# Eight experts and a two-layer product: weight conversion inside the second layer, and one block of rows completed by a one-hot product

## The chip, the cores and the metric

The kernel runs on one core of a Trainium2 chip. The metric is the device time of one execution in microseconds (us), given as the median of several runs. Beside the runs there is one execution recorded by the hardware profiler; all rows shown below come from that one.

## The reference, cut to what matters

Three parts follow one another. Attention keeps the 32 largest scores of each row (4 batches, 8 heads, 576 positions, head size 64) and gives a matrix `x` of 2304 rows by 512. Then each row with a positive skip score goes through the one of eight experts that its gate picks, and the last part is a product with two large matrices:

```python
for e in range(E):                       # E = 8, w1[e]: 512 x 1024, w2[e]: 1024 x 512
    mask = e_idx == e
    h = np.maximum(xc[mask] @ w1[e], 0.0)
    y[mask] = gate_w[mask, None] * (h @ w2[e])
out[do_compute] = xc + y
...
h = x @ w_in                             # 512 x 2048, float64
g = h * (1.0 / (1.0 + np.exp(-1.702 * h)))
return (g @ w_out).astype(np.float32)    # 2048 x 512, float64
```

`w_in` and `w_out` arrive as 64-bit floats. The kernel has to turn each of their elements into a pair of 32-bit floats, a high part and the rest.

## The kernel before, in words

Within a phase, each engine works through its instructions in the order in which the program writes them; nothing reorders them. A wait of one instruction therefore holds everything behind it on the same engine. Loads are issued by SP's queue, also in program order, and a load waits until the buffer that it fills is free.

**Attention** (lines 127 to 762) ends by writing the rows of `x` to two copies in device memory: XD, which the experts gather from, and X2D, which they scatter their results into and which the last part reads. It also sorts the experts by size and makes for each a list of row numbers, IXS. The four largest experts have up to 192 rows ("long", in two tiles of 128 and 64 rows), the other four up to 128 ("short"). They are taken in turn, long and short alternating: experts 0, 2, 4 and 6 in order of the work are long, 1, 3, 5 and 7 are short.

**An expert** (loop of line 990) goes so. `layer1` (line 922) multiplies the 1024 columns of w1, in eight steps f of 128, with the turned rows xgT. After each step ScalarE (ACT) makes the high part of hb, VectorE (DVE) the low part (line 930), and `step(f)` is called. There are four PSUM buffers `ph` for the eight steps. `step` (line 997) first splits one eighth of w2 into a high part (ACT) and a low part w2l (line 968: POOL in some steps, DVE in the others). In step 0 it has POOL gather the rows of the next expert (line 118). In steps 0 and 4 it scatters finished rows of the expert before (line 958). And it does the conversion of w_in: `split_f64` (line 859) is a generator in three parts. The first part loads a slice of 512 KB, named raw (line 861). The second is three VectorE instructions that put the bits of a 32-bit float together (lines 865 to 867). The third makes the high part on ACT (line 870) and the low part on POOL (line 871). There are sixteen slices of w_in; long experts convert three, short ones one. In step 0 the first two are loaded, and from step 2 on they are converted. There are two buffers for raw, so the third load waits until the first slice has been converted.

After layer 1 come, in program order: the loads of the next expert's w2 (eight pieces, line 106, each waiting until its buffer has been split), the turn of the next expert's rows (line 914, `turn`), and `layer2` (line 935), which multiplies hb with w2 in three products per step for a 128-row tile and two for the 64-row tile. VectorE then adds gate times result to the row (line 948, or 951 to 953 for the 64-row tile). The load of w1 for expert e+1 is written at the start of expert e (line 991), into one of two buffers.

**The seam** (lines 1021 to 1107): the last rows are scattered, two slices of w_out are loaded and converted, the table for the sigmoid is loaded, 31 products without use keep TensorE going (line 1028), and the experts' memory is given back. Then the first 512 rows of X2D are loaded (line 1046), turned by 16 transposes (line 1100) and split into xh and xl (lines 1103 to 1107).

**The product stage** (line 1109) takes the rows in blocks of 512. In each of 16 steps `up` makes phh (line 1067) and splits the activated result, and `down` (line 1082) multiplies the result of the step before with woh and wol. In the first block step f also converts slice f+2 of w_out.

Of the kernel before, what the change touches and what calls it, by code (L numbers as in the profile page):

```python
# [8 lines left out]
F32 = mybir.dt.float32  # L9
F32R = mybir.dt.float32r  # L10
# [19 lines left out]
def body(ctx: ExitStack, tc: tile.TileContext, q, k, v, w_skip, w_gate, w1, w2, w_in, w_out, out):  # L30
    nc = tc.nc
    V, A, G, T, SY = nc.vector, nc.scalar, nc.gpsimd, nc.tensor, nc.sync
    P = 128
# [57 lines left out]
    def load_w1(e):  # L91
        w1t = ew.tile([P, KC, F], F32, name="w1t")
        if isinstance(e, int):
            SY.dma_start(w1t, w1[e].rearrange("(c p) f -> p c f", p=P))
        else:
            SY.dma_start(w1t, w1[bass.ds(e, 1), :, :].rearrange("o (c p) f -> p (o c) f", p=P))
        return w1t
# [14 lines left out]
    own = cst.tile([P, 1], I32, name="own")  # L112
    V.tensor_copy(own, iop)
    IX0 = cst.tile([P, 2], I32, name="IX0")
    ZD = dram.tile([P, 8], F32, name="ZD")

    def fetch_rows(xg, ix, src=XD):
# [9 lines left out]
    with ExitStack() as ph:  # L127
# [116 lines left out]
        def warm(k):  # L244
            for _ in range(k):
                T.matmul(Y, ones[:, :P], ones, start=True, stop=True)
# [610 lines left out]
            first_rows()  # L857

    def split_f64(pool, src, hi, lo, queue=SY):
        raw = pool.tile([P, DFF // 4, 2], I32, name="raw")  # L860
        queue.dma_start(raw.rearrange("p n w -> p (n w)"), src.bitcast(I32))
        yield
        t = pool.tile([P, DFF // 4], I32, name="t")
        u = pool.tile([P, DFF // 4], I32, name="u")
        V.tensor_scalar(t, raw[:, :, 1], 3, 0x3FFFFFF8, op0=ALU.logical_shift_left, op1=ALU.bitwise_and)
        V.scalar_tensor_tensor(u, raw[:, :, 1], -0x40000000, t, op0=ALU.bitwise_and, op1=ALU.bitwise_or)
        V.scalar_tensor_tensor(t, raw[:, :, 0], 29, u, op0=ALU.logical_shift_right, op1=ALU.bitwise_or)
        yield
        wf = t.bitcast(F32)
        A.activation(hi, wf, AF.Copy)  # L870
        G.tensor_tensor(lo, wf, hi.bitcast(F32), op=ALU.subtract)
        yield
# [13 lines left out]
    with ExitStack() as ph:  # L886
# [21 lines left out]
        def turn(tiles, xgs):  # L908
            xgT = mp.tile([P, KC, NS], F32, name="xgT")
            o = 0  # L910
            for (_, rows), xg in zip(tiles, xgs):
                pt = pT.tile([P, KC, P], F32, name="pt")
                for c in range(KC):
                    T.transpose(pt[:, c, :rows], xg[:rows, c * P : (c + 1) * P], ident[:rows, :rows])
                if o:
                    A.activation(xgT[:, :, o : o + rows], pt[:, :, :rows], AF.Copy)
                else:
                    V.tensor_copy(xgT[:, :, :rows], pt[:, :, :rows])
                o += rows
            return xgT  # L920

        def layer1(w1t, xgT, ns, step):
# [9 lines left out]
                step(f)  # L932
            return hb

        def layer2(hb, ws, tiles, xgs):
            for (ix, rows), xg in reversed(list(zip(tiles, xgs))):
                py = pY.tile([P, DM], F32, name="py")
                xo = mp.tile([P, DM], F32, name="xo")
                if rows < P:
                    parts = [(P, 0), (P, 1)]  # L940
                else:
                    parts = [(0, 0), (0, 1), (2 * P, 0)]
                for f in range(FC1):
                    for u, (o, b) in enumerate(parts):
                        T.matmul(py, hb[:, f, o : o + P], ws[b][f], start=(f == 0 and u == 0),  # L945
                                 stop=(f == FC1 - 1 and u == len(parts) - 1))
                if rows == P:
                    V.scalar_tensor_tensor(xo, py, xg[:, DM:], xg[:, :DM], op0=ALU.mult, op1=ALU.add)  # L948
                else:
                    yo = mp.tile([P, DM], F32, name="yo", bufs=1)  # L950
                    A.activation(yo[:rows], py[rows:, :], AF.Copy)
                    V.tensor_tensor(yo[:rows], py[:rows, :], yo[:rows], op=ALU.add)
                    V.scalar_tensor_tensor(xo[:rows], yo[:rows], xg[:rows, DM:], xg[:rows, :DM], op0=ALU.mult, op1=ALU.add)
                late.append((ix, xo[:rows]))
# [18 lines left out]
        for c in range(KC):  # L973
            for u in range(4):
                us = slice(u * DFF // 4, (u + 1) * DFF // 4)
                todo.append(split_f64(wt, w_in[c * P : (c + 1) * P, us], wih[:, c, us], wil[:, c, us],
                                      SY if todo[1:] else A))

        turns = [0, 4, 1, 5, 2, 6, 3, 7]
        slots = []  # L980
# [6 lines left out]
        xgs = x0  # L987
        warm(10)
        nx = turn(slots[0], xgs)
        for e in range(E):  # L990
            w1n = load_w1(who[e + 1]) if e + 1 < E else None
            long = turns[e] < BIGS
            ns = NS if long else P
            convs = [todo.pop(0) for _ in range(1 if e % 2 else 3)]
            ws = ([], [])

            def step(f):
                split_w2(raws, ws, f, long)
                if f == 0:
                    for g in convs[:2]:  # L1000
                        next(g)
                    if e + 1 < E:
                        nxt.append(gather(slots[e + 1]))
                if f in (0, 4) and late:
                    scatter()
                for k, g in enumerate(convs):
                    if f - 2 * k in (2, 3):
                        next(g)
                if f == 4 and len(convs) > 2:
                    next(convs[2])  # L1010

            hs = layer1(w1t, nx, ns, step)
            if e + 1 < E:
                raws = load_w2(who[e + 1])
                nx = turn(slots[e + 1], nxt[-1])
            layer2(hs, ws, slots[e], xgs)
            if e + 1 < E:
                xgs = nxt[-1]
                w1t = w1n

        while late:
            scatter()
        todo = [out_weights(fw, wt) for _ in range(2)]
        for _ in range(3):
            for g in todo:
                next(g)
        A.activation(padf, padf, AF.Sigmoid)
        warm(31)

    ewx.close()  # L1030
    with ExitStack() as ph:
        ph.enter_context(tc.manual_schedule())
        fw = ph.enter_context(tc.tile_pool(name="fw2", bufs=1))
        wt = ph.enter_context(tc.tile_pool(name="wt2", bufs=2))
        fp = ph.enter_context(tc.tile_pool(name="fp", bufs=2))
        pT = ph.enter_context(tc.tile_pool(name="pT", bufs=2, space=PSUM))
        pH = ph.enter_context(tc.tile_pool(name="pH", bufs=2, space=PSUM))
        pO = ph.enter_context(tc.tile_pool(name="pO", bufs=1, space=PSUM))
        todo = [None, None] + [out_weights(fw, wt) for _ in range(2, FC2)]
        blocks = [(t0, min(512, NT - t0)) for t0 in range(0, NT, 512)]  # L1040

        def fetch(b):
            t0, n = blocks[b]
            xr = fp.tile([P, 4, DM], F32, name="xr", bufs=1)
            for t in range(n // P):
                SY.dma_start(xr[:, t, :], X2D[t0 + t * P : t0 + (t + 1) * P, :])  # L1046
            xh = fp.tile([P, KC, 512], F32R, name="xh")
            xl = fp.tile([P, KC, 512], F32R, name="xl")
            return xr, xh, xl

        def flip(b, x, c):
            n = blocks[b][1]
# [38 lines left out]
                    V.tensor_copy(ot, po[t])  # L1091
                SY.dma_start(out[t0 + t * P : t0 + (t + 1) * P, :], ot)

        x = fetch(0)
        for f in range(2, 4):
            next(todo[f])
        pts = [pO.tile([P, DM], F32, name=f"po{c}") for c in range(KC)]
        for t in range(4):
            for c in range(KC):
                T.transpose(pts[c][:, t * P : (t + 1) * P], x[0][:, t, c * P : (c + 1) * P], ident)  # L1100
        for c in range(KC):
            if c == 1:
                V.tensor_copy(x[1][:, c, :], pts[c])
# [1 line left out]
                A.activation(x[1][:, c, :], pts[c], AF.Copy)  # L1105
        for c in range(KC):
            V.tensor_tensor(x[2][:, c, :], pts[c], x[1][:, c, :].bitcast(F32), op=ALU.subtract)
        prev = None
        for b in range(len(blocks)):
            po = [pO.tile([P, DM], F32, name=f"po{t}") for t in range(blocks[b][1] // P)]  # L1110
            for f in range(FC2):
                gs = up(b, x, f)
                if b == 0 and f + 2 < FC2:
                    next(todo[f + 2])
                    next(todo[f + 2])
                    if f + 4 < FC2:
                        next(todo[f + 4])
                if prev:
                    down(*prev)
                    if prev[0] < b:  # L1120
                        flush(prev[0], prev[3])
                prev = (b, f, gs, po)
                if b + 1 < len(blocks):
                    if f == 1:
                        xn = fetch(b + 1)
                    elif f in (6, 8, 10, 12):
                        flip(b + 1, xn, f // 2 - 3)
            if b + 1 < len(blocks):
                x = xn
# [32 lines left out]
```

## Time and profile before

| | us |
|---|---|
| median of 3 runs | 1116.03 (1115.49 to 1120.85) |
| the profiled execution, its own time | 1116.85 |
| its span | 1115.0 |
| TensorE busy (PE) | 1017.0, 91% of the span |
| VectorE busy (DVE) | 706.9, 63% |
| ScalarE busy (ACT) | 622.1, 56% |
| GpSimd busy (POOL) | 449.0, 40% |

The span is what the profiler saw from first to last instruction. The profiler's names are PE for TensorE's products and PEld for its weight loads, DVE, ACT, POOL and SP. An `L` number is a line of the kernel. In an arrow `out<-in` the names are those of the program. A row of a timeline gives start, duration, engine, line, instruction and count; in brackets stand the idle time before it and what ended that. `hb <- ACT` in a wait reads: the instruction that writes hb waited for ACT. "Clk" is the clock granted to TensorE as a share of its full rate. In float32, TensorE's timeline has two records for each product.

### The profile page before, as it was taken

To read this page: it belongs to the slowest core of one execution; us is meant where nothing else is said; L and a number is where in the kernel's file an instruction comes from. 1 tells how busy PE (TensorE), PEld (TensorE's weight loads), DVE (VectorE), ACT (ScalarE), POOL (GpSimd) and SP (SyncE) were. 2 spreads that over 40 slices of the span, in tenths; PEclk is the share of its full clock that TensorE was granted. 3 is DMA by queue.
4 is the path that set the end of the run, shared out by engine and by line. 5 is a ranking of instruction groups with operands and counts; after the bars stand their busy time and mean duration, and the time that the engine had idled before them with its cause. 6 is when DMAs were issued, how large, how long until landed. Compare 5 with 4: busy or idle time off the path is not lost. (4 is left out here: it accounts for less than half of the span.)

```text
span 1115.0 us, 20235 instructions
## 1 busy us (share of the span) xinstructions
PE 1017.0 (91%) x6523; PEld 848.8 (76%) x6523; DVE 706.9 (63%) x3376; ACT 622.1 (56%) x1426; POOL 449.0 (40%) x584
## 2 busy tenths in 40 slices
PE   6899999899999999877879778999999999999998
PEld 3777777787777777765768667688888878888887
DVE  7988889988998899944655666566322223222232
ACT  5999999999999999932233333333222222222232
POOL 4777777767777777713435354222000000000000
PEclk8999999999999999988889889999999999999999
DMA  4211141154111310036677673332100010010010
GB/s 102 48 33 33 32 119 29 36 187 122 37 37 37 83 54 16 2 86 212 225 258 275 231 245 134 136 120 95 59 18 1 19 58 1 1 57 1 0 39 19
DMA packets 98803, 91.86 MB, mean 82 GB/s; under 512 B 71680, under 2 KB 71680, under 8 KB 98688
## 3 DMA queue, kind: packets, MB, share of 16 engines
q1 hardware_dynamic: 96704, 84.17, 24.6%
q0 software_dynamic: 1696, 5.25, 1.4%
q8 instruction: 54, 0.88, 0.3%
q10 hardware_dynamic: 288, 1.05, 0.3%
q14 instruction: 61, 0.50, 0.2%
HBM read 72.38 MB, written 17.05 MB: 80 GB/s over the span
## 5 line engine op out<-in xcount | busy, mean ns | idle before, releaser
L275 DVE MAX8 C<-s 128x8 f32<-128x72 f32 x1152 | 217.9, 221 | 2.2 <-ACT s L268 2.2
L307 POOL TENSOR_TENSOR z<-s,z 128x576 f32<-128x576 f32 x144 | 203.2, 1411 | 4.3 <-ACT z L302 4.0
L1070 DVE TENSOR_TENSOR g<-phh,g 128x512 f32<-128x512 f32 (+1 forms) x80 | 51.1, 638 | 178.8 <-ACT g L1069 178.8
L1069 ACT ACTIVATE g<-phh 128x512 f32<-128x512 f32 (+1 forms) x80 | 44.3, 553 | 168.0 <-PE phh L1067 168.0
L409 PE MATMUL Y<-vn,AT 128*128 128x65 f32 x1024 | 121.4, 272 | 0.0
L409 PEld LDWEIGHTS Y<-vn,AT 128*128 128x128 f32 x1024 | 119.4, 192 | 0.0
L302 ACT ACTIVATE z<-s,T 128x576 f32<-128x576 f32 x144 | 116.4, 808 | 2.8 <-DVE T L291 2.8
L339 ACT ACTIVATE k<-s,BT 128x576 bf16<-128x576 f32 x144 | 115.3, 801 | 0.4
L1082 PE MATMUL po<-woh,gh 128*128 128x512 f32 x288 | 112.7, 391 | 1.9 <-DVE ot L1091 1.7
L353 PE MATMUL pt<-ident,a 128*128 128x128 f32 x576 | 113.1, 283 | 1.2 <-POOL z L307 1.0
L268 ACT ACTIVATE s<-SS 128x576 f32<-128x576 f32 x144 | 96.8, 673 | 30.7 <-PE SS L262 28.6
L1082 PE MATMUL po<-wol,gh 128*128 128x512 f32 x288 | 112.4, 390 | 0.0
L1082 PE MATMUL po<-woh,gl 128*128 128x512 f32 x288 | 112.3, 390 | 0.0
L334 POOL TENSOR_SCALAR a<-s,BT 128x576 f32<-128x576 f32 x144 | 107.3, 745 | 0.5 <-POOL BT L296 0.4
L312 DVE MAX8 z<-z 128x8 f32<-128x576 f32 x144 | 107.0, 743 | 0.0
L354 PE MATMUL pt<-nident,k 128*128 128x128 bf16 x576 | 105.1, 221 | 0.0
L927 PE MATMUL ph<-xgT,w1t 128*128 128x192 f32 (+1 forms) x512 | 76.9, 312 | 17.8 <-DVE hb L930 17.2
L260 PE MATMUL SS<-kT,qT 64*128 64x256 f32 x512 | 73.6, 407 | 19.6 <-ACT s L268 19.6
L353 PEld LDWEIGHTS pt<-ident,a 128*128 128x128 f32 x576 | 83.8, 146 | 9.4 <-POOL z L307 1.2
L342 ACT ACTIVATE AT<-pt 128x512 f32<-128x512 f32 x144 | 89.8, 623 | 0.2 <-PE pt L354 0.2
L927 PEld LDWEIGHTS ph<-xgT,w1t 128*128 128x128 f32 x512 | 74.2, 198 | 20.0 <-issue 17.6
L1074 DVE TENSOR_TENSOR gl<-g,gh 128x512 fp32r<-128x512 f32 (+1 forms) x80 | 51.2, 639 | 52.5 <-ACT gh L1072 47.1
(233 smaller groups left out, 2151.8 us busy)
## 6 DMA issues: line engine op xcount, KB each, us to landing
w1t<-in_moe_w_dram SPq DMA_DIRECT2D x8, 2048.0 KB, 8.5
w<-in_moe_w_dram SPq DMA_DIRECT2D x64, 256.0 KB, 3.4
raw<-in_moe_w_out_dram SPq DMA_DIRECT2D x16, 512.0 KB, 3.3
raw<-in_moe_w_in_dram SPq DMA_DIRECT2D x14, 512.0 KB, 8.9
xr<-X2D SPq DMA_DIRECT2D x18, 256.0 KB, 3.7
out_dram<-ot SPq DMA_DIRECT2D x18, 256.0 KB, 2.2
qn<-in_q_dram SPq DMA_DIRECT2D x32, 128.0 KB, 2.9
kn<-in_k_dram SPq DMA_DIRECT2D x32, 128.0 KB, 2.9
```

The source lines that it names most:

```text
L268: A.activation(s, SS[:, SLOT[j] : SLOT[j] + S], AF.Copy, scale=SC)
L275: V.max(C[:, g, :], s[:, g * SEG : (g + 1) * SEG])
L302: A.activation(z, d["s", c], AF.Sign, bias=T24[:, n, 7:8], scale=-1.0 - 2.0 ** -20, accum_out=sg)
L307: G.tensor_tensor(z, d["s", c], z, op=ALU.mult)
L312: V.max(z8, d.pop(("z", c)))
L334: G.tensor_scalar(a[:, o : o + S], d.pop(("s", c)), BT[:, n, :1], 1.0, op0=ALU.add, op1=ALU.mult)
L339: A.activation(d["k", r][:, o : o + S], d["s", c], AF.Relu, bias=BT[:, n, 1:], scale=-BIG)
L353: T.matmul(out, a, ident, is_transpose=True, start=True, stop=False)
L354: T.matmul(out, d["k", r][:, sl], nident, start=False, stop=True)
L409: T.matmul(y[:, w * j : w * j + w], t[:, 4 * j + g, :], d["v"][:, g, j, :], start=False, stop=(j == 1 and g == 3))
L927: T.matmul(ph_[:, :ns], w1t[:, c, f * P : (f + 1) * P], xgT[:, c, :ns], start=(c == 0), stop=(c == KC - 1))
L1082: T.matmul(po[t], lh[:, ts_], rh[f], start=(f == 0 and u == 0), stop=(f == FC2 - 1 and u == 2))
```

## The change

The conversion of w_in leaves `step` and stands behind the turn, ahead of `layer2`. Its slices are loaded one expert ahead, with three buffers for raw, and its temporary `u` is gone. The load of w1 is written after layer 1, two experts ahead. In the last expert, the first 512 rows of X2D are loaded in step 2, before this expert's rows are scattered. Its gated result is kept apart as `delta`. A matrix `spot`, made of a row of running numbers and a compare with the expert's row numbers, has a one where a row of the block is one of the expert's rows. Four products of delta with spot then add the missing part onto the transposes in PSUM. One slice of w_out is converted in the last expert instead of two behind it; the others follow one step ahead of their use. The products without use are gone.

```diff
-        raw = pool.tile([P, DFF // 4, 2], I32, name="raw")
+        raw = pool.tile([P, DFF // 4, 2], I32, name="raw", bufs=3)
...
-        u = pool.tile([P, DFF // 4], I32, name="u")
...
-        V.scalar_tensor_tensor(u, raw[:, :, 1], -0x40000000, t, op0=ALU.bitwise_and, op1=ALU.bitwise_or)
-        V.scalar_tensor_tensor(t, raw[:, :, 0], 29, u, op0=ALU.logical_shift_right, op1=ALU.bitwise_or)
+        V.scalar_tensor_tensor(t, raw[:, :, 1], -0x40000000, t, op0=ALU.bitwise_and, op1=ALU.bitwise_or)
+        V.scalar_tensor_tensor(t, raw[:, :, 0], 29, t, op0=ALU.logical_shift_right, op1=ALU.bitwise_or)
...
-                if rows == P:
+                if end:
+                    end["delta"] = delta = ew.tile([P, DM], F32, name="w2_1", bufs=1)
+                    V.tensor_scalar(delta, py, xg[:, DM:], None, op0=ALU.mult)
+                    G.tensor_tensor(xo, delta, xg[:, :DM], op=ALU.add)
+                elif rows == P:
...
-                                      SY if todo[1:] else A))
+                                      SY if c or u > 2 else A))
...
+        def take(e):
+            gs = [todo.pop(0) for _ in range(1 if e % 2 else 3)]
+            for g in gs:
+                next(g)
+            return gs
+
+        w1s = [w1t, load_w1(who[1])]
+        ahead = take(0)
         for e in range(E):
-            w1n = load_w1(who[e + 1]) if e + 1 < E else None
...
-                if f == 0:
-                    for g in convs[:2]:
-                        next(g)
-                    if e + 1 < E:
-                        nxt.append(gather(slots[e + 1]))
-                if f in (0, 4) and late:
+                if f == 0 and e + 1 < E:
+                    nxt.append(gather(slots[e + 1]))
+                if f in ((0, 4) if e + 1 < E else (0, 1)) and late:
                     scatter()
-                for k, g in enumerate(convs):
-                    if f - 2 * k in (2, 3):
-                        next(g)
-                if f == 4 and len(convs) > 2:
-                    next(convs[2])
+                if e + 1 == E and f == 1:
+                    V.tensor_copy(last_ix, IXS[:, turns[e], :1])
+                elif e + 1 == E and f == 2:
+                    end["rows"] = ew.tile([P, KC, F], F32, name="w1t")
+                    for t in range(4):
+                        SY.dma_start(end["rows"][:, t, :DM], X2D[t * P : (t + 1) * P, :])
+                    end["spot"] = spot = ew.tile([P, DM], F32, name="w2_0", bufs=1)
+                    G.iota(spot, pattern=[[1, DM]], base=0, channel_multiplier=0, allow_small_or_imprecise_dtypes=True)
+                elif e + 1 == E and f == 4:
+                    V.tensor_scalar(end["spot"], end["spot"], last_ix, None, op0=ALU.is_equal)
 
-            hs = layer1(w1t, nx, ns, step)
+            hs = layer1(w1s.pop(0), nx, ns, step)
+            convs = ahead
             if e + 1 < E:
                 raws = load_w2(who[e + 1])
                 nx = turn(slots[e + 1], nxt[-1])
+            if e + 2 < E:
+                w1s.append(load_w1(who[e + 2]))
+            if e + 1 == E:
+                first_out = out_weights(fw, wt)
+                next(first_out)
+            for g in convs:
+                next(g)
+                next(g)
+            if e + 1 < E:
+                ahead = take(e + 1)
+            else:
+                for _ in range(2):
+                    next(first_out)
+                A.activation(padf, padf, AF.Sigmoid)
             layer2(hs, ws, slots[e], xgs)
...
-        todo = [out_weights(fw, wt) for _ in range(2)]
-        for _ in range(3):
-            for g in todo:
-                next(g)
-        A.activation(padf, padf, AF.Sigmoid)
-        warm(31)
...
-        x = fetch(0)
-        for f in range(2, 4):
-            next(todo[f])
+        x = [end["rows"], *room()]
         pts = [pO.tile([P, DM], F32, name=f"po{c}") for c in range(KC)]
-        for t in range(4):
-            for c in range(KC):
-                T.transpose(pts[c][:, t * P : (t + 1) * P], x[0][:, t, c * P : (c + 1) * P], ident)
+        for c in range(KC):
+            for t in range(4):
+                T.matmul(pts[c][:, t * P : (t + 1) * P], x[0][:, t, c * P : (c + 1) * P], ident, is_transpose=True,
+                         start=(t == 0), stop=False)
+        for c in range(KC):
+            T.matmul(pts[c], end["delta"][:, c * P : (c + 1) * P], end["spot"], start=False, stop=True)
...
+        ewx.close()
+        fw2 = ph.enter_context(tc.tile_pool(name="fw2", bufs=1))
+        wt2 = ph.enter_context(tc.tile_pool(name="wt2", bufs=2))
+        todo = [None, out_weights(fw, wt2)] + [out_weights(fw2, wt2) for _ in range(2, FC2)]
+        for f in range(1, 4):
+            next(todo[f])
...
-                if b == 0 and f + 2 < FC2:
-                    next(todo[f + 2])
-                    next(todo[f + 2])
+                if b == 0 and f + 1 < FC2:
+                    next(todo[f + 1])
+                    next(todo[f + 1])
```

## Rows read from the trace of the kernel before

**Rows 1.** Windows: length, busy PE, PEld, DVE, ACT, POOL, granted clock, DMA share, GB/s.

```profile
512.71:696.72 184.01, 152.74 (x808) 131.76 (x809) 115.21 (x202) 62.70 (x151) 82.05 (x65) 0.91 0.69 236
707.78:1115.00 407.22, 401.57 (x1880) 334.47 (x1880) 144.50 (x232) 113.37 (x201) 18.11 (x14) 1.00 0.11 37
```

**Rows 2.** Waits, 512 to 697 us.

```profile
DVE t L865 <- DMA raw<-in_moe_w_in_dram: 24.2, 4, 8.0
...
PE ph L927 <- DVE hb L930: 17.2, 5, 6.0
...
PE py L945 <- DVE hb L930: 7.4, 5, 1.7
...
PE pt L914 <- DMA xg<-XD,IXS: 3.8, 3, 1.9
...
PE py L945 <- DVE w2l L968: 2.0, 4, 0.7
```

**Rows 3.** Timeline of PE, 495 to 760 us: first layers, one turn, warm-up.

```profile
512.71 9.37 PE L927 MATMUL ph<-xgT,w1t 128*128 128x192 f32 x56 [0.60 <-ACT xgT L916]
...
539.57 7.31 PE L927 MATMUL ph<-xgT,w1t 128*128 128x128 f32 x64
548.80 1.43 PE L914 MATMUL pt<-ident,xg 128*128 128x128 f32 x8 [1.92 <-DMA xg<-XD,IXS]
...
556.84 9.26 PE L927 MATMUL ph<-xgT,w1t 128*128 128x192 f32 x56
570.03 2.90 PE L927 MATMUL ph<-xgT,w1t 128*128 128x192 f32 x8 [3.92 <-DVE hb L930]
...
587.09 7.30 PE L927 MATMUL ph<-xgT,w1t 128*128 128x128 f32 x64
...
602.36 9.28 PE L927 MATMUL ph<-xgT,w1t 128*128 128x192 f32 x56
...
634.74 7.31 PE L927 MATMUL ph<-xgT,w1t 128*128 128x128 f32 x64
...
650.04 9.29 PE L927 MATMUL ph<-xgT,w1t 128*128 128x192 f32 x56
...
682.17 6.41 PE L927 MATMUL ph<-xgT,w1t 128*128 128x128 f32 x56
...
696.72 6.87 PE L898 MATMUL pt<-ones 128*128 128x512 bf16 x31
```

**Rows 4.** Chain of waits, 500 to 720 us, in order of time.

```profile
697.95 2.72 DMA X2D<-xo,IXS
...
707.13 0.61 ACT xh L1105
...
707.78 6.04 PE phh L1067 x24
713.82 2.75 PE po L1082 x12
```

**Rows 5.** Timeline of SP's queue, around expert 2.

```profile
555.13 14.77 SPq L861 DMA_DIRECT2D raw<-in_moe_w_in_dram  x3
```

**Rows 6.** Timeline of DVE, experts 1 and 2.

```profile
547.46 3.85 DVE L968 TENSOR_TENSOR w2l<-w,w2h 128x512 fp32r<-128x512 f32 x1 [0.23 <-ACT w2h L967]
...
567.66 0.43 DVE L865 TENSOR_SCALAR t<-raw 128x512 int32<-128x512 int32 x1 [5.94 <-DMA raw<-in_moe_w_in_dram]
...
568.86 0.69 DVE L867 SCALAR_TENSOR_TENSOR t<-raw,u 128x512 int32<-128x512 int32 x1
...
571.93 1.64 DVE L866 SCALAR_TENSOR_TENSOR u<-raw,t 128x512 int32<-128x512 int32 x1
```

**Rows 7.** Timeline of POOL, expert 2.

```profile
570.29 1.33 POOL L871 TENSOR_TENSOR wil<-t,wih 128x512 fp32r<-128x512 f32 x1 [5.61 <-ACT wih L870]
```

**Rows 8.** Tile xg, 605 to 609 us: the gather in expert 4.

```profile
L118 POOL DMA_INDIRECT xg<-XD,IXS x1: 1382/1382/1382, 606.2 to 606.2; - x1
...
DMA to landing us min/median/max: 8.0/8.0/8.0
```

More of the change, by code (lines that the diff above doesn't have):

```diff
@@ L114, in body @@
     IX0 = cst.tile([P, 2], I32, name="IX0")
+    last_ix = cst.tile([P, 1], F32, name="last_ix")
     ZD = dram.tile([P, 8], F32, name="ZD")
@@ L933, in layer1 @@
             return hb
+        end = {}
         def layer2(hb, ws, tiles, xgs):
@@ L989, in body @@
         nx = turn(slots[0], xgs)
+        def take(e):
[5 more added lines that the diff above has]
+        ahead = take(0)
         for e in range(E):
-            w1n = load_w1(who[e + 1]) if e + 1 < E else None
             long = turns[e] < BIGS
             ns = NS if long else P
-            convs = [todo.pop(0) for _ in range(1 if e % 2 else 3)]
             ws = ([], [])
@@ L1018, in body @@
                 xgs = nxt[-1]
-                w1t = w1n
         while late:
             scatter()
-        todo = [out_weights(fw, wt) for _ in range(2)]
-        for _ in range(3):
-            for g in todo:
-                next(g)
-        A.activation(padf, padf, AF.Sigmoid)
-        warm(31)
-    ewx.close()
     with ExitStack() as ph:
         ph.enter_context(tc.manual_schedule())
-        fw = ph.enter_context(tc.tile_pool(name="fw2", bufs=1))
-        wt = ph.enter_context(tc.tile_pool(name="wt2", bufs=2))
         fp = ph.enter_context(tc.tile_pool(name="fp", bufs=2))
@@ L1038, in body, with room @@
         pO = ph.enter_context(tc.tile_pool(name="pO", bufs=1, space=PSUM))
-        todo = [None, None] + [out_weights(fw, wt) for _ in range(2, FC2)]
         blocks = [(t0, min(512, NT - t0)) for t0 in range(0, NT, 512)]
+        def room():
+            return [fp.tile([P, KC, 512], F32R, name=nm) for nm in ("xh", "xl")]
         def fetch(b):
@@ L1046, in fetch @@
                 SY.dma_start(xr[:, t, :], X2D[t0 + t * P : t0 + (t + 1) * P, :])
-            xh = fp.tile([P, KC, 512], F32R, name="xh")
-            xl = fp.tile([P, KC, 512], F32R, name="xl")
-            return xr, xh, xl
+            return xr, *room()
         def flip(b, x, c):
```

## The prediction, made before the changed kernel was built

> **What bounds the kernel now.** The windows come first. The product stage (from 707.78 us to the end) has a busy TensorE at full granted clock; only edits to its start can count there. The expert stage, 512.71 to 696.72 us, has TensorE busy 152.7 of 184.0 us at a granted clock of 0.91 and the DMA engines at a share of 0.69 [rows 1]. So time can come only from this stage and the seam of 11.1 us behind it.
>
> The waits say what stops TensorE there: 17.2 us for hb in layer 1, 7.4 us for hb in layer 2, 3.8 us for gathered rows, 2.0 us for w2l [rows 2]. hb is made by VectorE, and VectorE's own longest wait is 24.2 us, four times, for raw, the w_in slices [rows 2]: its conversion is queued between two hb instructions of layer 1, so when the slice is late, hb is late, and TensorE stops.
>
> TensorE's timeline gives each expert's length as the distance between starts of layer 1: 26.9, 17.3, 30.3, 15.3, 32.4, 15.3, 32.1 and, to the warm-up, 14.5 us [rows 3]. The long ones (192 rows, even) carry three conversions, the short ones one.
>
> What would each cost without a stop? 56 records of long layer 1 take 9.26 us, so 64 take 10.6; short, 7.3; eight row transposes 1.4 [rows 3]. Twelve 512-column matmuls take 2.75 us, 0.229 each [rows 4], so layer 2 is 9.2 (40 of them) or 5.5 (24). Long: 10.6 + 0.7 + 9.2 = 20.5. Short: 7.3 + 1.4 + 5.5 = 14.2. Last: 12.8. The rest is **excess**: long 6.4, 9.8, 11.9, 11.6 (39.7 together); short 3.1, 1.1, 1.1 (5.3); last 1.7.
>
> The order on VectorE and SP shows why the long ones lose most. In expert 2, raw was issued at 555.13 behind a whole w1, the third slice held SP for want of a buffer, 14.8 us for the three issues [rows 5], and the first landed when VectorE resumed at 567.66 after 5.94 us of idling [rows 6]. TensorE stopped 3.92 us for hb, and the eight records after it took 2.90 us in place of 1.3 [rows 3]: they ran at the lower of the two clocks, 1.2 GHz.
>
> **The change part by part.**
>
> *Conversions to layer 2.* In layer 1 VectorE no longer waits for raw, so the hb stops and the slow clock after them go: at most the long excess, 39.7 us. In layer 2 the slice has arrived: the first landed 10.8 us after layer 1 began [rows 3, 6], layer 2 begins 11.3 us after, and the third slice, no longer held back, adds about 1.5 us (512 KB at the stage's burst rate, an estimate above its mean of 236 GB/s [rows 1]), while it is wanted 4 us into layer 2. The SP order of the large loads stays: w2 of e+1, w1 of e+2, slices of e+1. The name "two ahead" moves w1 past nothing; the third raw buffer is what frees SP, so w2 starts with the first free buffer.
>
> Does the work fit in layer 2? A conversion is 0.43 + 0.69 + 0.69 us of VectorE [rows 6], so 5.4 for three, behind some 2.6 us of leftovers (an estimate: the last hb, w2l and the turn copy at up to 0.7 each, and their waits), in 9.9 us; yo and xo follow. It is not free of POOL: w2l took 3.85 us and a conversion step 1.64 in place of 0.69 while POOL subtracted [rows 6], and one subtraction takes 1.33 [rows 7]. I charge two subtractions per long expert, 2.6 us. VectorE then ends some 3.5 us into the next layer 1. Four ph buffers of 0.91 us each in a short layer 1 cover 3.65, so I take 0.3 us per short expert; bounds 0 and 3.
>
> The Trainium skill (SBUF — State Buffer, Who interferes with whom) speaks against this placement: VectorE and GpSimd share a pair of ports, an instruction with two SBUF inputs locks out a GpSimd one that reads SBUF and the reverse, and the loser fully blocks. By that rule all three subtractions may block, 1.3 us more per long expert, some 4 us in all; without it the charge would be nothing. The 3.85 us above agree with a full block.
>
> *What is late next.* The gathered rows. POOL issues the gather in step 0 of layer 1, which does not move. In expert 4 it was issued 3.9 us after layer 1 began and landed 8.0 us later [rows 8], at 11.9, where an undisturbed layer 1 ends at 10.6: a wait of 1.3 that the hb stop hides today. I take it for each long expert with 0.4 us of slower clock: excess 1.7, so 6.8 of the 39.7 remains. **Gain 32.9.** Bounds: nothing left, or the rival below. The short experts already wait for it (3.8 us in three [rows 2]); busier DMA engines add perhaps 0.5 each. With the 0.3 above: **loss 2.4.** The last expert loses its conversion stop and gains a 512-wide iota, a compare and an earlier scatter: excess 1.7 to 0.7, **gain 1.0.** Three slices on ACT's queue instead of two put one issue more ahead of the first hb; TensorE has four ph buffers there, so I charge nothing.
>
> *The seam.* Today: 11.06 us from 696.72 to 707.78, filled by the last scatter (2.72 us), the row loads and the transposes [rows 4]. The rows now load under the last expert without its part; on SP they wait for the two scatters of expert 6, and only w_out's first slice is queued behind them. The last expert's own addition moves to POOL, and its scatter is wanted by the second block alone, over 5 us later. In their place stand, in VectorE's queue, a conversion of w_in and one of w_out (3.6 us) ahead of delta (about 0.7, as any 512-wide step), so delta comes some 4 us after layer 2; the 16 transposes fit before. Then four fp32 products of 512 columns. Long layer 1 does 192 columns in two records, 0.33 us, so 0.88 each, 3.5 together. Then a copy of 0.61 [rows 4] and issue: 4 + 3.5 + 1 = 8.5. **Gain 2.6.** Bounds: delta at once, the transposes' 2.9 us (twice the eight above) ahead, 7.0, gain 4.1; w_out's slice late by 3 us, 12, loss 1. Table load, w_out and the 31 warm-up products lie beside this; TensorE stays busy enough that I charge no clock.
>
> *The product stage* converts w_out one step ahead of its use instead of two. A step is over 5 us, the chain 1.8 + 0.6 + 1.3: hidden. The in-place temporaries cost nothing, since those steps ran in sequence already.
>
> Sum: 32.9 - 2.4 + 1.0 + 2.6 = 34.1. The profiled execution took 1116.85 us (span 1115.0), giving 1082.8; the median is 0.8 below it, so 1082.
>
> **The rivals.**
>
> *A, nothing is late next.* Gathers land in time once SP no longer bunches the loads; VectorE never spills. Left over: long 0.3 each, short 0.3 each, last 0.7, in all 2.8 of 46.7, and the seam 7.0. Gain 43.9 + 4.1 = 48.0: 1068. For it: the DMA engines have a share of 0.69, and short experts' gathers wait little. Against: the same bytes in 140 us need 310 GB/s. Chance 0.22.
>
> *B, gathers take the place of hb.* If the landing of 8.0 us holds in short experts too, their second gather (issued some 5 us in) lands at 13 against an end at 7.3: 5.7 and 1.2 of slow clock, 21 in three; in long experts 2.5 each, 10. Excess left 32 of 46.7, seam gain 2: 1099. For it: rows 8; against: the loads pile up mainly in long layer 1. Chance 0.15.
>
> *C, slower: the slice is late in layer 2.* VectorE then stands before yo, xo and the next expert's hb. Today 24.2 us of this wait cost 39.7 of excess, 1.64 for 1. Slower by over 0.5% (what a measurement of this kernel can tell from no change) needs 4 x 1.64 x d above 34.1 + 5.6, so d above 6 us in each long expert. At 6.7 us: 1082 + 44 = 1126. The point is a slice landing 19 us after layer 1 begins in place of 12; only w2's 2 MB ahead of it would do that, and it is queued behind. Chance 0.04.
>
> *D, no effect:* the DMA engines already limit the stage as a whole, and TensorE waits elsewhere. 1116; a share of 0.69 speaks against. Chance 0.02.
>
> **How the numbers follow.** Forecast 0.57 at 1082, A 0.22, B 0.15, C 0.04, D 0.02. The range 1064 to 1101 takes in A and B with some of their error. Faster by over 0.5%: 0.57 + 0.22 + 0.14 = 0.93; within: 0.03; slower: 0.04.
>
> **What would show it.** Right: VectorE's wait for raw gone from layer 1; long experts near 22 us; TensorE's waits led by xg; granted clock above 0.95 in the stage; 8 to 9 us from the last layer 2 to the first phh. Wrong: raw waits in layer 2, hb waits in short experts over 1 us, or delta more than 6 us behind layer 2.

## The result, and the profile after

The changed kernel takes 1086.15 us (median of 4 runs, 1084.86 to 1087.12) against 1115.76 us of the kernel before in the same comparison: a ratio of 0.973, interval 0.970 to 0.976. The forecast was 1082 in a range of 1064 to 1101. The profiled execution took 1087.12 us, its span is 1085.3 us, 29.7 us less than before.

The windows of the changed kernel: the expert stage, the seam (here and below counted from the start of the last layer-2 record to the first phh; before, that is 11.30 us, 0.24 more than the prediction's count), and the product stage. Columns as in [rows 1].

```profile
515.89:666.51 150.62, 138.81 (x808) 124.16 (x808) 114.12 (x203) 65.67 (x150) 80.95 (x65) 0.98 0.81 290
666.51:678.54 12.03, 6.95 (x27) 4.56 (x25) 4.72 (x8) 3.40 (x6) 4.73 (x4) 0.86 0.13 50
678.54:1085.30 406.76, 401.64 (x1881) 334.27 (x1880) 146.10 (x234) 114.12 (x202) 19.39 (x15) 1.00 0.12 41
```

The expert stage lost 33 us of its 184 [rows 1], its clock rose from 0.91 to 0.98, and the same bytes now pass at 290 GB/s. The product stage is as it was, and the seam has not become shorter.

TensorE's timeline of the changed kernel, experts 0 to 3 (first layers, and the first three turns with what they waited for), answers to [rows 3]:

```profile
515.89 10.67 PE L927 MATMUL ph<-xgT,w1t 128*128 128x192 f32 x64 [0.60 <-ACT xgT L916]
528.16 0.63 PE L914 MATMUL pt<-ident,xg 128*128 128x128 f32 x4 [1.60 <-DMA xg<-XD,IXS]
537.75 7.31 PE L927 MATMUL ph<-xgT,w1t 128*128 128x128 f32 x64
546.78 1.04 PE L914 MATMUL pt<-ident,xg 128*128 128x128 f32 x8 [1.73 <-DMA xg<-XD,IXS]
554.96 10.56 PE L927 MATMUL ph<-xgT,w1t 128*128 128x192 f32 x64
566.34 0.63 PE L914 MATMUL pt<-ident,xg 128*128 128x128 f32 x4 [0.81 <-DMA xg<-XD,IXS]
575.91 7.31 PE L927 MATMUL ph<-xgT,w1t 128*128 128x128 f32 x64
```

Each of these first layers is one unbroken group of 64 records. Before, the long ones came as 56 and 8 records with up to 6 us between them. All lengths from the starts of layer 1 (the last expert: to its last layer-2 record), beside the prediction's undisturbed ones:

| us | before | after | undisturbed, by the prediction |
|---|---|---|---|
| long (0, 2, 4, 6) | 26.86, 30.25, 32.38, 32.13 | 21.86, 20.95, 21.33, 21.99 | 20.5 |
| short (1, 3, 5) | 17.27, 15.27, 15.30 | 17.21, 17.41, 14.61 | 14.2 |
| last (7) | 14.31 | 15.26 | 12.8 |
| seam | 11.30 | 12.03 | |

The waits of the changed kernel, 512 to 680 us, answer to [rows 2]:

```profile
PE pt L914 <- DMA xg<-XD,IXS: 9.8, 7, 1.9
...
PE po L1117 <- DVE w L951: 5.1, 1, 5.1
```

VectorE's 24.2 us for the w_in slices and TensorE's 17.2 and 7.4 us for hb are gone. In their place stand the gathered rows, 9.8 us in all seven turns (before 3.8 in three), and one wait of 5.1 us in the seam: the transposes (L1117) wait for delta (L951, which the trace calls `w` after its memory).

The last expert and the seam, VectorE's timeline of the changed kernel, cut to the rows that the text needs:

```profile
661.20 2.74 DVE L1024 TENSOR_SCALAR w<-w,last_ix 128x512 f32<-128x512 f32 x1 [4.45 <-POOL w L1022]
...
665.66 0.41 DVE L865 TENSOR_SCALAR t<-raw 128x512 int32<-128x512 int32 x1
...
668.82 0.98 DVE L865 TENSOR_SCALAR t<-raw 128x512 int32<-128x512 int32 x1 [1.30 <-DMA raw<-in_moe_w_out_dram]
...
671.18 0.74 DVE L951 TENSOR_SCALAR w<-py,xg 128x512 f32<-128x512 f32 x1
677.63 0.69 DVE L1123 CAST xh<-po 128x512 fp32r<-128x512 f32 x1 [5.71 <-DMA X2D<-xo,IXS]
```

and TensorE's of the same stretch:

```profile
664.79 0.50 PE L947 MATMUL py<-w2l,hb 128*128 128x512 f32 x1 [1.35 <-DVE w2l L974]
...
666.51 0.39 PE L947 MATMUL py<-w2h,hb 128*128 128x512 f32 x1
671.98 3.38 PE L1117 MATMUL po<-ident,w1t 128*128 128x128 f32 x16 [5.08 <-DVE w L951]
675.20 3.60 PE L1120 MATMUL po<-w,w 128*128 128x512 f32 x8
678.54 1.49 PE L1086 MATMUL phh<-xh,wih 128*128 128x512 f32 x4
```

VectorE stands idle for 4.45 us around the end of the last expert's layer 1, because the compare (L1024) is written ahead of the last hb steps and waits for GpSimd's iota. The compare then takes 2.74 us, and w2l behind it makes TensorE wait 1.35 us in layer 2. Behind layer 2, a conversion of w_in and one of w_out, whose slice is late by 1.30 us, stand ahead of delta; the transposes begin 0.06 us after delta's end. The first copy into xh (L1123), which reads what the transposes and products made, waited until 677.63 for the landing of the last scatter.

### The profile page after: what moved, and what is told of

It is laid out like the page before. It is cut to its first block, busy times and chain, and to the rows that moved or that the text cites. A ratio compares the mean times of both kernels' runs of the same rounds, so it can differ in the third digit from the quotient of the medians.

```text
span 1085.3 us, 20202 instructions
## 1 busy us (share of the span) xinstructions
PE 1006.2 (93%) x6500; PEld 845.3 (78%) x6500; DVE 706.3 (65%) x3378; ACT 626.1 (58%) x1426; POOL 450.2 (41%) x586
## 5 line engine op out<-in xcount | busy, mean ns | idle before, releaser
L1086 PE MATMUL phh<-xh,wih 128*128 128x512 f32 (+1 forms) x320 | 80.7, 374 | 0.0
L1091 ACT ACTIVATE gh<-g 128x512 fp32r<-128x512 f32 (+1 forms) x80 | 47.2, 590 | 56.3 <-DVE g L1089 56.3
```

What stands on the lines that cost most here:

```text
L1086: T.matmul(phh[:, :n], lh[:, c, fs], rh[:, c, :n], start=(u == 0 and c == 0), stop=(u == 2 and c == KC - 1))
```

## The experiments

Unless said otherwise, each starts from the changed kernel ("after"), and ratios are to the kernel before.

### Is it the place, the third buffer, or both?

The third buffer alone, in the kernel before (u gone as well):

```diff
-        raw = pool.tile([P, DFF // 4, 2], I32, name="raw")
+        raw = pool.tile([P, DFF // 4, 2], I32, name="raw", bufs=3)
```

> The kernel before with the third raw buffer and without u, conversions left in layer 1. My theory, that their place between two hb instructions is what stops TensorE: VectorE still waits for raw in the long experts, they stay at 28 to 32 us, and the time within 6 us of 1116. The rival, that the held-up SP queue is the cause: long experts 21 to 24 us and a time of 1085 to 1095.

Measured: 1120.43 us, ratio 1.0037 (1.0010 to 1.0064). Its waits, 505 to 705 us:

```profile
DVE t L864 <- DMA raw<-in_moe_w_in_dram: 25.6, 4, 8.1
PE ph L926 <- DVE hb L929: 18.6, 5, 6.1
```

These are the rows of before [rows 2] over again. SP is no longer held (the three raw issues in expert 2 take 1.45 us in place of 14.77 [rows 5]), but the slice still comes too late for a place inside layer 1.

The old place with the new loading (three buffers, loads one expert ahead); the added loop stands in `step`:

```diff
-            hs = layer1(w1s.pop(0), nx, ns, step)
             convs = ahead
+            hs = layer1(w1s.pop(0), nx, ns, step)
...
-            for g in convs:
-                next(g)
-                next(g)
...
+                for k, g in enumerate(convs):
+                    if f - 2 * k in (2, 3):
+                        next(g)
```

> The changed kernel with the conversions put back into layer 1 (step 2 on), slices still loaded one expert ahead. Place is the cause: in the long experts slices land 9 to 14 us after their issue, 7 to 12 us into layer 1, but are wanted 4 us in, so VectorE waits 3 to 8 us for raw, hb stops come back and the time is 1105 to 1120. Loading ahead is the cause: 1084 to 1092.

Measured: 1118.42 us, ratio 1.0016 (0.9986 to 1.0045). Its waits, 505 to 705 us:

```profile
DVE t L865 <- DMA raw<-in_moe_w_in_dram: 25.2, 6, 8.9
PE ph L927 <- DVE hb L930: 16.6, 6, 6.8
```

So loading ahead and a buffer more bring nothing where the conversion stays in layer 1. Slices loaded earlier still, two experts ahead, were not tried in the old place. This kernel also has the whole one-hot part of the change, and that part brings nothing here either.

The new place with two buffers, the third slice loaded once the first is converted:

```diff
-        raw = pool.tile([P, DFF // 4, 2], I32, name="raw", bufs=3)
+        raw = pool.tile([P, DFF // 4, 2], I32, name="raw", bufs=2)
...
-            for g in gs:
+            for g in gs[:2]:
                 next(g)
...
             for g in convs:
                 next(g)
                 next(g)
+                if g is not convs[-1] and g is convs[0]:
+                    next(convs[2])
```

> The changed kernel with two raw buffers in place of three: a long expert's third slice is loaded when the first has been converted, in layer 2, and converted behind the others. Theory (the place needs the third buffer: a slice takes some 11 us to land in this stretch, and layer 2 has some 9): VectorE waits 3 to 8 us for the third slice in each of the four long experts, that holds up the short expert's first layer behind it, TensorE waits for hb there, and 10 to 20 us of the gain go: 1096 to 1106. Rival (the four ph buffers and the slice's own queue cover it): 1086 to 1089, no hb waits.

Measured: 1102.13 us (1099.42 to 1104.57), ratio 0.986 (0.982 to 0.990); 16.0 us of the gain of 29.6 are gone. Its waits, 505 to 700 us:

```profile
DVE t L865 <- DMA raw<-in_moe_w_in_dram: 21.5, 3, 7.8
PE ph L927 <- DVE hb L930: 18.2, 4, 7.0
```

and TensorE's timeline shows where they lie. Three of the four hb waits, 4.42 to 7.04 us, are in the short expert behind a long one (here expert 3); in the last expert 0.24 us is left:

```profile
578.31 3.73 PE L927 MATMUL ph<-xgT,w1t 128*128 128x128 f32 x32
589.08 5.73 PE L927 MATMUL ph<-xgT,w1t 128*128 128x128 f32 x32 [7.04 <-DVE hb L930]
```

The four ph buffers are used up (32 records are four steps), then TensorE stops, and the second half takes 5.73 us in place of 3.73, at a granted clock of 0.66 (589 to 595 us). **Place and buffer pay only together.** This is also the prediction's rival C made real: a slice late in layer 2 is paid for in the next layer 1.

### What is late next: the gathered rows

(Run e4_gather_ahead.) Each expert's rows gathered one expert earlier, ahead of layer 2, and those of expert 1 ahead of the loop (five xg buffers; yo shares xo to make room):

```diff
-                xg = ew.tile([P, DM + 1], F32, name="xg", bufs=4)
+                xg = ew.tile([P, DM + 1], F32, name="xg", bufs=5)
...
-                if f == 0 and e + 1 < E:
-                    nxt.append(gather(slots[e + 1]))
...
+        nxt.append(gather(slots[1]))
...
             if e + 2 < E:
+                nxt.append(gather(slots[e + 2]))
                 w1s.append(load_w1(who[e + 2]))
```

> The changed kernel with each expert's rows gathered one expert earlier (in layer 2 of the expert two before), a fifth buffer for them. Theory: the gathers are what is late now, 9.8 us of TensorE's waits and some 3 us of slow clock after three of them, so long experts come to 20.3, short ones to 14.2, and the time falls by 9 to 13 us to 1073 to 1077. Rival, the weight loads are the limit and another DMA wait takes their place: a gain under 4 us.

Measured: 1075.03 us (1074.08 to 1076.96), ratio 0.963 (0.959 to 0.968), 11.1 us below after. TensorE's timeline:

```profile
534.17 7.69 PE L927 MATMUL ph<-xgT,w1t 128*128 128x128 f32 x64
...
541.70 0.99 PE L914 MATMUL pt<-ident,xg 128*128 128x128 f32 x8
548.26 10.56 PE L927 MATMUL ph<-xgT,w1t 128*128 128x192 f32 x64
558.65 0.60 PE L914 MATMUL pt<-ident,xg 128*128 128x128 f32 x4
568.20 7.68 PE L927 MATMUL ph<-xgT,w1t 128*128 128x128 f32 x64
```

No turn waits any more. Long experts take 20.0 us, short ones 14.1 to 14.4, and the window from 514.13 to 653.50 us has the full clock:

```profile
514.13:653.50 139.37, 135.79 (x808) 122.05 (x808) 109.24 (x203) 64.83 (x150) 81.55 (x64) 1.00 0.87 312
```

So what stood above the undisturbed lengths in after was the gather's latency and the clock behind it, not bandwidth: the same transfers now pass at a DMA share of 0.87. The last expert, whose end this edit leaves as in after, took 16.66 us, 1.4 more, with a stop of 0.77 us for hb that after does not have. In after the clock shows behind the wait of 1.73 us in expert 1 (windows of after):

```profile
546.50:548.00 1.50, 1.22 (x9) 0.98 (x10) 1.50 (x1) 0.14 (x1) 1.11 (x1) 1.00 0.39 71
548.00:550.00 2.00, 2.00 (x7) 1.59 (x7) 2.00 (x3) 0.25 (x1) 1.78 (x2) 0.66 0.96 304
550.00:552.00 2.00, 2.00 (x6) 1.54 (x6) 1.93 (x3) 0.00 (x0) 0.50 (x1) 0.50 0.83 242
```

### The end of the last expert and the seam

(Run e11_old_tail.) The conversion moved, the end left as it was before (two w_out slices behind layer 2, rows loaded after the last scatter, warming products, no one-hot product):

```diff
-                if end:
-                    end["delta"] = delta = ew.tile([P, DM], F32, name="w2_1", bufs=1)
...
-                first_out = out_weights(fw, wt)
...
+        todo = [out_weights(fw, wt) for _ in range(2)]
...
+        warm(31)
```

> The changed kernel with only the conversion moved: the end of the MoE stage and the start of the product stage are those of the kernel before (rows fetched after the last scatter, two w_out slices converted behind layer 2, warming matmuls, no one-hot product). Theory (the one-hot product brought nothing, since its stretch measured 11.8 us against 11.1 before): 1085 to 1086.5, ratio 0.973. Rival (the prediction's own terms, 2.6 us for that stretch and 1.0 for the last expert): 1089 to 1090.

Measured: 1084.94 us (1084.65 to 1088.77), ratio 0.972 (0.969 to 0.975): no difference to after that can be measured. The rival of 1089 to 1090 counts the last expert's 1.0 us for the one-hot part; in the prediction it comes from the conversion's leaving, which this kernel keeps. Without it the prediction's terms make 1088.8 (the seam's 2.6 us above after), and five of the six runs lie below 1087. From the last layer 1 to the first phh it takes 25.80 us, before 25.61, after 27.29. The expert itself has 12.39 us of this in this kernel (before 14.31, so the conversion's leaving gave it 1.9) and 15.26 in after: what the one-hot part adds to it costs 2.9. The seam has 13.41, so the one-hot part gave back 1.4 there.

Now the same end rearranged (run e3_both): the compare made in expert 6, and the w_out conversion behind layer 2, after delta:

```diff
-                for _ in range(2):
-                    next(first_out)
                 A.activation(padf, padf, AF.Sigmoid)
             layer2(hs, ws, slots[e], xgs)
+            if e + 1 == E:
+                for _ in range(2):
+                    next(first_out)
...
+            if e + 2 == E:
+                rows_t = ew.tile([P, KC, F], F32, name="w1t")
+                spot = rows_t[:, 0, DM:]
+                G.iota(spot, pattern=[[1, DM]], base=0, channel_multiplier=0, allow_small_or_imprecise_dtypes=True)
...
```

> The changed kernel with the conversion of w_out put behind delta, and spot made during expert 6 in the unused half of the row tile. Theory: the seam is set by delta, which stood behind a wait for the iota (4.5 us), a compare held up by POOL (2.7 us) and a conversion waiting for its slice, so the seam falls from 11.8 to 7 to 8 us and the last expert by 1 to 2: 1086 to 1080 or 1081. Rival, the transposes wait for the loaded rows or for the last scatter: seam stays above 10 us and the time within 2 us of 1086.

Measured: 1085.88 us (1082.36 to 1088.94), ratio 0.974 (0.969 to 0.979): a miss. TensorE's timeline says why:

```profile
661.76 0.55 PE L1118 MATMUL po<-ident,w1t 128*128 128x128 f32 x3 [1.34 <-DVE w L951]
663.12 2.50 PE L1118 MATMUL po<-ident,w1t 128*128 128x128 f32 x13 [0.81 <-DMA w1t<-X2D]
665.42 4.46 PE L1121 MATMUL po<-w1t,w 128*128 128x512 f32 x8
672.15 1.48 PE L1087 MATMUL phh<-xh,wih 128*128 128x512 f32 x4 [2.27 <-ACT xh L1126]
```

Layer 2 ended here at 660.04; delta comes at once, the wait for it falls from 5.08 to 1.34 us, and the last expert is 1.4 us shorter (13.90). But the seam still takes 12.11: now the copies into xh hold phh. They waited for the last scatter (ScalarE's row), which stood on GpSimd behind wol, the subtraction of the late w_out slice (GpSimd's rows):

```profile
671.50 1.57 ACT L1126 ACTIVATE xh<-po 128x512 fp32r<-128x512 f32 x3 [4.54 <-DMA X2D<-xo,IXS]
...
667.03 1.26 POOL L871 TENSOR_TENSOR wol<-t,woh 128x512 fp32r<-128x512 f32 x1 [2.76 <-ACT woh L870]
668.45 0.98 POOL L964 DMA_INDIRECT X2D<-xo,IXS  x1 [0.15 <-POOL wol L871]
```

The copies don't read what is scattered. What the two have in common is memory: xh is the first tile of a pool opened after the experts' pools are given back, and xo, which the scatter reads, is in one of those. Three further steps test that.

First the scatter ahead of the w_out conversion (run e7_scatter_first):

```diff
             if e + 1 == E:
+                scatter()
                 for _ in range(2):
                     next(first_out)
```

> The kernel of e3_both with one thing changed: on GpSimd the last expert's scatter is issued ahead of the last steps of the w_out conversion. Theory (the first use of the next phase's SBUF pool, the xh copies, waits until everything in the old pools is done, and that is the last scatter's landing): in e3_both the scatter ran at 668.45, 4.1 us after the sum it writes was ready (664.3), and landed about 671.2; now it lands near 667, before the products end (669.9 there), so phh starts about 0.8 us behind the products: 1.5 us less between layer 2 and phh (11.9 to about 10.4), the copies' wait for X2D gone, time 1084.4 against 1085.9. Rival (the copies are held by something else in the tail, such as wol's subtraction or TensorE's half clock): 11.9 us and 1085.9 stay.

Measured: 1079.94 us (1077.72 to 1083.06), ratio 0.967 (0.964 to 0.970). The wait for X2D is gone and the seam takes 9.06 us, 3.05 less and more than the 1.5 expected. The two medians lie 5.9 us apart, which the seam explains only in part. The two profiled spans differ by 1.2 us only, because in this one expert 6 took 24.23 us against 21.23, with a wait of 2.46 us for its gathered rows; what makes up the rest between the medians is not shown. ScalarE's row shows who is the new last one, wol:

```profile
671.28 1.33 ACT L1127 ACTIVATE xh<-po 128x512 fp32r<-128x512 f32 x2 [1.38 <-POOL wol L871]
```

Then the first w_out slice loaded ahead of the rows (run e9_load_first; the line that takes the slice up later is left out):

```diff
                 if e + 1 == E and f == 2:
+                    end["out"] = out_weights(fw, wt)
+                    next(end["out"])
```

> e7_scatter_first with the load of w_out's first slice issued ahead of the load of the first 512 rows in SP's queue. Theory (TensorE's 16 transposes, 8 products and the copies are then the whole distance): w_out's conversion comes early and holds nothing any more; 10 us from the last layer-2 matmul to phh, time 1084.0 to 1084.5. Rival (the raw slice delays the rows, on which the transposes waited 0.8 us in e3_both): transposes wait 1.5 us or more for the rows, time 1085 to 1086.

Measured: 1079.65 us (1077.09 to 1083.15), ratio 0.967 (0.963 to 0.970), not to be told from the step before; seam 8.89 us in place of the 10 expected. All 16 transposes go through in 1.97 us, with no wait for the rows, and the scatter's landing is the last again (1.77 us of wait ahead of phh).

Then this and the earlier gathers in one kernel (run e10_best; the diffs of both):

> e9_load_first and e4_gather_ahead in one kernel. Theory (the two gains lie in different stretches and add): long experts 20.0 us, short 14.2, the seam as in e9_load_first, time 1072.5 to 1074 against 1075.0 for e4_gather_ahead. Rival (the gathers moved ahead delay the rows or the scatter in the seam): 1075 or more.

Measured: **1069.87 us** (1068.31 to 1073.91), ratio 0.959 (0.956 to 0.962): the fastest of all, and better than the sum expected. Its seam, TensorE's timeline:

```profile
653.23 2.24 PE L1120 MATMUL po<-ident,w1t 128*128 128x128 f32 x16 [1.33 <-DVE w L951]
655.30 3.60 PE L1123 MATMUL po<-w1t,w 128*128 128x512 f32 x8
660.42 1.48 PE L1089 MATMUL phh<-xh,wih 128*128 128x512 f32 x4 [1.52 <-ACT xh L1128]
```

Its last layer-2 record starts at 651.50, so the seam is 8.92 us. Last, the same with the last sum kept in memory that is not given back:

```diff
-                xo = mp.tile([P, DM], F32, name="xo")
+                xo = end["rows"][:, 1, DM:] if end else mp.tile([P, DM], F32, name="xo")
```

> e10_best with the last expert's sum kept in the free half of the row tile, so that no tile of the old pools is read by the last scatter. Theory (in e10_best phh waits 1.5 us for the copies and these for the scatter's landing, because the new pool's first use waits for the old pools' last reader): the copies' wait for X2D is gone, phh starts about 0.7 us behind the products, 8.9 us from layer 2 to phh become 7.7; time 1068 to 1069.5 against 1069.9. Rival (the copies then wait for wol's subtraction on GpSimd, which ended at 659.0 there, as the products did): 8.9 us stay within 0.4.

Measured: 1070.91 us (1068.03 to 1072.69), ratio 0.959 (0.956 to 0.962), not to be told from the kernel without it. The seam takes 8.18 us, between what the two theories gave. ScalarE's and TensorE's rows:

```profile
659.96 1.58 ACT L1128 ACTIVATE xh<-po 128x512 fp32r<-128x512 f32 x3 [1.52 <-POOL wol L871]
...
660.61 1.48 PE L1089 MATMUL phh<-xh,wih 128*128 128x512 f32 x4 [0.64 <-ACT xh L1128]
```

The scatter was issued at 657.51, 4.16 us behind delta as in the kernel without this edit (4.15). There it was issued at 656.58 and landed 2.9 us later, and the first copy began at 659.59. Here too it took 2.9 us, so it landed at about 660.4, and the copies began at 659.96, before that: this shows the memory to be the link. They wait for wol instead, whose temporary lies in a pool of the experts too; that this is the reason for that wait was not tested.

## Why the prediction was right, and where it was not

By the profiled executions, the spans differ by 29.7 us, and the prediction's sum was 34.1:

| term | forecast, us | measured, us |
|---|---|---|
| long experts | -32.9 | -35.5 |
| short experts | +2.4 | +1.4 |
| last expert | -1.0 | +0.95 |
| seam | -2.6 | +0.7 |
| product stage | 0 | -0.5 |
| start of the first layer 1 | 0 | +3.2 |

**Right, and shown.** The bound: conversion inside layer 1 cost the long experts their excess. With the place put back and everything else kept, the time of before returns, and the long experts take 117.8 us together (before 121.6, after 86.1). The third buffer: without it 16 of 29.6 us go. What is late next: the gathered rows; the prediction took 1.3 us of wait for each long expert, and the four turns behind a long layer 1 waited 1.60, 0.81, 1.20 and 1.86 us, on average 1.37. Taking the waits of all seven turns away brings 11.1 us. The spill of VectorE into the next layer 1 was 2.4 us in the first short expert (it took up hb at 540.19; layer 1 had begun at 537.75), forecast 3.5, and no hb wait followed.

The long term came out 2.6 us better mainly because the undisturbed length was set too high: 20.0 us without the gather waits, not 20.5. In the short experts the waits grew by 0.5 us in all (4.29 against 3.8), less than the 0.5 each. Of the 6.6 us that they kept above the undisturbed 14.2, 4.3 are wait; behind the two longer waits the clock was lower.

The price for VectorE and GpSimd in each other's way was of the right kind. In the first long expert of after two conversion steps took 1.66 and 1.67 us in place of 0.69, about 2 us in all where the prediction charged 2.6. The costliest block was one that the prediction did not price, the compare of 2.74 us. It began 0.1 us after the first of two subtractions of GpSimd and ended 0.3 us after the second (first row). In the kernel e7_scatter_first, where it stands in expert 6 and GpSimd is idle beside it, the same compare takes 0.49 us (second row; its matrix lies in the memory of w1t there):

```profile
661.10 2.54 POOL L974 TENSOR_TENSOR w2l<-w,w2h 128x512 fp32r<-128x512 f32 x2
...
640.34 0.49 DVE L1032 TENSOR_SCALAR w1t<-w1t,last_ix 128x512 f32<-128x512 f32 x1
```

The Trainium skill (SBUF — State Buffer, Who interferes with whom) says that the loser blocks for the other's whole instruction, and that a step of this form, too, can ask for the ports that both share, when its operands allow. The 2.74 us agree, and they show the block to last over two subtractions in a row.

**Wrong: the seam.** The step that failed is "delta comes some 4 us after layer 2; the 16 transposes fit before". Delta began 4.67 us after the last layer-2 record started, and 5.47 passed until the transposes began (5.2 by the prediction's count), over a microsecond more than the sum's 4. The transposes did not fit before: they waited 5.08 us for it, although it is no operand of theirs, and then took 3.38 us, at a clock of 0.50 for their first 2 us, where the prediction charged no clock (1.97 us at a clock of 1.00 in e9_load_first). In after and in all eight of its variants with a one-hot product the first transpose starts within 0.1 us of delta's end. Delta reads py, and the banks that the transposes write come from pools that are opened when py's pool is given back. That this is the reason is argued from those rows; transposes written into banks held from earlier were not tried. In place of the 8.5 us forecast (delta 4, products 3.5, copy and issue 1), delta with 5.5, the transposes behind it with 3.2 and the products with the copy beside them with 3.3 make the 12.03 measured. A second statement of this step failed too: that the last scatter "is wanted by the second block alone". The copies of the first block wait for its landing, in after until 677.63, while the products were still running, so that it held nothing there; in e3_both, with delta early, this wait held phh and the seam stayed at 12.11.

**Wrong: the last expert.** The step left an excess of 0.7 us with "a 512-wide iota, a compare and an earlier scatter" in it; measured against the same 12.8, it is 2.5. The cost was in the queues: GpSimd's second scatter went only after 2.45 us of idling, at 658.34; the iota stood behind it (660.56), the compare behind the iota, and three hb steps behind the compare. Without the whole one-hot part (run e11_old_tail) the last expert is 2.9 us shorter.

These two make 5.3 us too little, and the better expert terms give 3.6 back. So the total came nearer than its terms, and that part is luck; the signs named for the experts (long ones near 22 us, waits led by xg, a clock above 0.95) came, the 8 to 9 us for the seam did not. The start of the first layer 1, 3.2 us later than before, is left to the run: over the twelve profiles it lies between 512.46 and 517.02 us, and the latest is the kernel before with only a buffer more.

**The rivals.** B (gathers at 5.7 us in short experts) did not come: no turn waited over 1.9 us. A (gathers in time by themselves) did not come in the changed kernel, whose turns waited 9.8 us, but its 1068 named the right remainder: with the gathers early and the seam put in order the kernel takes 1069.87. D is out. C's mechanism is real, as the kernel with two buffers shows, but the third buffer keeps it away.

## What to carry to other kernels

Put work that depends on a late load where the engine that does it has slack, and give it the buffer that lets the load leave early: here the buffer alone was worth nothing and the place alone about half. When a queue's stop is removed, ask at once what is late next and whether that can be issued a stage earlier for the price of a buffer. And where one phase's memory is given back to the next, look at who reads the old memory last: here the first copies of the new phase waited for a scatter that they share no data with, so order such a reader first, not last.

## What was not expected of the hardware

A stop of 1.73 us on TensorE was followed by some 4 us at a lower clock (0.66 and 0.50 in the windows from 548 to 552 us), although TensorE was busy throughout them: with it expert 1 took 3.0 us more than the undisturbed 14.2. The wait of 0.74 us in expert 5 left 14.61 us. But the length of the stop alone does not decide it. In after, the turn of expert 6 waited 1.86 us and the clock stayed at 1.00 (642 to 650 us). In e11_old_tail a turn that waited 1.69 us was followed by 1.00 (expert 3 took 15.55 us), and one that waited 1.61 us by 0.50 between 624 and 626 us (expert 5 took 17.12 us). What decides it is not shown here. And the DMA engines carried 312 GB/s over the whole expert stage when nothing waited on a single gather, against 236 GB/s before: a share of 0.69 was no sign of a limit.
